# Gelu's result left in PSUM, kv's sums read from PSUM, a second exponent tile in dead weights' place, and three last blocks of 128, 384 and 256 tokens

## The chip, the cores and the metric

The kernel runs on one core of a Trainium2 chip. The core has five engines that each work through their own instructions in the order in which they were written: TensorE (PE, with its weight loads shown apart as PEld), VectorE (DVE), ScalarE (ACT), GpSimd (POOL) and SyncE (SP), which here issues the DMAs. Engines wait for each other through semaphores. SBUF is the large on-chip memory; PSUM is the small one of eight banks into which TensorE writes its products. The metric is the device time of one execution in microseconds.

## The reference: what is computed

FAVOR+ attention (random features) feeds a two-layer network. All inputs are float32, and q is drawn 4.675 times larger than k.

```python
batch, n_heads, seq, head_dim = (8, 8, 576, 64); n_features = 128
def phi(x):
    h = einsum('bhsd,md->bhsm', x, omega) - sum(x * x) / 2
    return exp(h - max(h, axis=-1)) / sqrt(m)          # x is q or k, times 64 ** -0.25
kv, z = einsum('bhsm,bhsd->bhmd', k_p, v), sum(k_p, axis=2)
num, den = einsum('bhsm,bhmd->bhsd', q_p, kv), einsum('bhsm,bhm->bhs', q_p, z) + 1e-06
x = (num / den) rearranged to 4608 tokens x 512
out = gelu(x @ w_in) @ w_out                           # 512 -> 2048 -> 512
```

## The kernel before

**Attention** goes by units: one unit is a pair of heads of one batch, so there are 32, four per batch. Its tokens sit in nine tiles of 128 for k and as four pieces of 288 columns for q. The first four units (batch 0) and the next four (batch 1) use plain float32. The 24 units of batches 2 to 7 (mode 2) use products split into a high and a low part:

- `x_high` (ACT, L295) rounds a piece of k or q, `x_low` (POOL, L301) makes the rest, `proj` and `proj_q` (PE, L308 and L336) multiply by omega into a PSUM bank of the kind `at`, of which there are three.
- For k, `proj_lo` (ACT, L313) and `proj_add` (DVE, L319, L320) add the halves into the tile `et` and take row maxima. For q, `q_blocks` (DVE, L344, L346) transposes into `et`. `k_shift` (POOL, L325) and `q_shift` (DVE, L371) subtract the maxima.
- `exps` (ACT, L379) takes the exponential of the whole of `et` in one instruction with a table load on either side of it.
- `q_back`, `q_high`, `q_low` (L386, L391, L395) transpose q's exponentials back and split them. `k_high` (POOL, L432) and `k_low` (DVE, L440) split k's into `kh` and `kl`, two buffers each, for five groups of tiles. `kv` (PE, L459) multiplies them with v, which `v_a` to `v_d` on POOL (L402, L408, L414, L420) have split into `vb`; the sums stand in one `at` bank.
- `kv_a` (ACT, L468) copies the bank's columns behind the first 64 to `kvs`; `kv_b` (DVE, L475, L476) adds the partial sums, the first time with both operands in SBUF; ACT's L477 and L483 and DVE's L487 (`kvl`) finish the weights. `num` (PE, L527), `den` (ACT, L536, L537) and `div` (DVE, L544 to L555) write the tokens into tiles `xs`.

**The network** goes by 12 blocks of 384 tokens, each in 16 chunks of 128 hidden columns. Block 0 is plain float32. For the rest, `block_max` to `block_scales` find a block's scale, and `block_high` (ACT, L687) and `block_low` (DVE, L692) split its tokens. A chunk is: `mm1` (PE, 12 matmuls at L714) into one of two `h` banks; `act_high` on ACT, Gelu from PSUM into the SBUF tile `g` (L726) and the high half `gh` (L727); `act_low` on DVE, `gl` (L732); and two chunks later `mm2` (PE, L748 to L750), nine matmuls into three `acc` banks. At a block's end `store` (DVE, L761) scales an `acc` bank into `o`, of which there are two buffers, and SP sends it out (L762).

**The order** of all this is written out by hand: every step is entered at a time `at(t, ...)`, in steps of which a chunk has six, the numbers stand in the table `X`, and a sort of the entries gives the order of the instructions on every engine. A mode-2 unit is placed every 34 to 36 steps, so about six chunks go with each; that spacing is the same before and after the change. The numbers only set an order: an engine takes its next instruction as soon as what it waits for is there.

Of the kernel before, what the change touches and what calls it, by code (L numbers as in the profile page):

```python
# [8 lines left out]
F32 = mybir.dt.float32  # L9
# [18 lines left out]
X = dict(pk=-27.0, dk=1.68, pq=-16.0, dq=2.67, xh=-4.13, xl=-2.56, plo=0.04, padd=1.37, ksh=1.5,  # L28
         qb=1.05, qm=3.26, dqm=0.12, load=-1.8, v=-14.43, dv=2.66, kh=2.57, kl=5.15, kv=6.56, dkv=1.38,
         kva=12.3, dkva=0.41, qback=7.69, qhigh=8.95, qlow=9.94, dqb=2.92, num=18.13, dnum=4.27,  # L30
         den=0.87, div=1.67, b0=110.11, b1=33.21, b2=349.2, b3=36.0, ah=4.03, al=6.26, m2=3.13,
         dm2=1.16, st=3.16, bm=-15.41, bm1=-9.64, bh=6.05, dbh=0.99, bl=2.82, m10=5.35, m11=20.5,
         mf=-13.0, mf1=4.09, mf2=7.5, mkv=5.5, mkz=7.55, mqt=8.28, mdq=1.0, mnum=17.0, mdn=4.0,
         wi=-27.37, wis=5.9, wo=5.31, wo0=0.56, wsi=72.19, wso=91.0, wss=4.24, ci=68.1, co=86.32,
         we=3.7, we0=6.27, e0=9.0, e1=2.0, e2=6.0, e3=7.3, e4=7.0, e5=10.69, lag=2, we_n=8)
# [3 lines left out]
def favor_attention_ffn(ctx: ExitStack, tc: tile.TileContext, qT, kT, v, omT, w_in, w_out, out):  # L39
# [15 lines left out]
    NTT = T // P  # L55
    NBLK = NTOK // T
# [30 lines left out]
    et = cp.tile([P, 2 * NT, M], F32, name="et")  # L87

# [225 lines left out]

    def proj_add(u, i):
        t0, t1 = XG[i][0] // P, XG[i][1] // P
        own.update({('e', t): u for t in range(t0, t1)})
        es = et[:, t0:t1]
        nc.vector.tensor_tensor(es, u.pp.pop(i)[:, 0:t1 - t0, 0], u.lo.pop(i)[:, 0:t1 - t0], op=ALU.add)  # L319
# [9 lines left out]
    ef = et.rearrange("p t m -> p (t m)")  # L329
    eq = ef[:, R2:].rearrange("p (n r) -> p n r", r=32)  # L330
# [8 lines left out]
    def q_blocks(u, g):  # L339
        own['q', g] = u  # L340
# [3 lines left out]
        nc.vector.transpose(ef[:, slice(*XG[NK + g])], u.pp.pop(NK + g)[:, 0:HS])  # L344
        s = slice(g * QB, (g + 1) * QB)
        nc.vector.tensor_reduce(u.mx[:, s], eq[:, s], axis=AX.X, op=ALU.max)  # L346
# [21 lines left out]
    def q_shift(u):  # L368
        need((u, 'nq'))
        has(u, *[('q', g) for g in range(4)])  # L370
        nc.vector.tensor_tensor(eq, eq, u.nq.unsqueeze(2).broadcast_to([P, 4 * QB, 32]), op=ALU.add)  # L371
        done.add((u, 'q'))

    def exps(u):
        if u.mode == 2:
            need((u, 'k'), (u, 'q'))
        has(u, *[('e', t) for t in range(NT)])
        has(u, *([('e', t) for t in range(NT, 2 * NT)] if u.mode == 1 else [('q', g) for g in range(4)]))
        nc.scalar.activation(et, et, AF.Exp)  # L379
# [13 lines left out]
    def q_low(u, g):  # L393
        u.ql[g] = p2().tile([P, HS], F32R, tag="ql", name="ql", bufs=4)
        (nc.gpsimd if g == 1 else nc.vector).tensor_tensor(  # L395
            u.ql[g], u.qt.pop(g), u.qh[:, g * HS:(g + 1) * HS], op=ALU.subtract)

    def v_a(u):
# [3 lines left out]
        nc.gpsimd.tensor_scalar(vb[:, :, 0:D], u.v, 1.0, 1.0, op0=ALU.mult, op1=ALU.mult)  # L402
# [7 lines left out]
    def v_c(u):  # L410
# [3 lines left out]
        nc.gpsimd.tensor_scalar(vb[:, :, D:2 * D], u.v, 1.0, 1.0, op0=ALU.mult, op1=ALU.mult)  # L414
# [10 lines left out]
    def k_high(u, g):  # L425
        need((u, 'e'))
        has(u, *[('e', t) for t in KG[g]])
        n = len(KG[g])
# [3 lines left out]
        nc.gpsimd.tensor_scalar(kh[:, :n], es, KSC, 1.0, op0=ALU.mult, op1=ALU.mult)  # L432
        u.kk[g] = (kh, kl)

    def k_low(u, g):
        has(u, *[('e', t) for t in KG[g]])
        n = len(KG[g])
        kh, kl = u.kk[g]
        es = et[:, KG[g][0]:KG[g][0] + n]
        nc.vector.scalar_tensor_tensor(kl[:, :n], es, KSC, kh[:, :n], op0=ALU.mult, op1=ALU.subtract)  # L440
        done.add((u, 'kl', g))

    def kv(u, g):
# [3 lines left out]
        has(u, 'v')  # L447
# [3 lines left out]
        kh, kl = u.kk.pop(g)  # L451
        for i, t in enumerate(KG[g]):
            for hh, ti in parts(t):
# [3 lines left out]
                ops = [(kh, VW), (kl, 2 * D + 1)]  # L457
                for x, (k, w) in enumerate(ops if f else ops[::-1]):
                    nc.tensor.matmul(o[:, 0:w], k[:, i], vb[:, ti, 0:w], start=f and x == 0, stop=end and x == 1,  # L459
# [4 lines left out]
    def kv_a(u):  # L464
        need(*[(u, 'kv', g) for g in range(len(KG))])
        u.kvs = sp.tile([P, 2, VW - D], F32, tag="kvs", name="kvs", bufs=1)
        u.pkv = u.pk[:, 0:2 * VW].rearrange("p (h w) -> p h w", h=2)
        nc.scalar.copy(u.kvs, u.pkv[:, :, D:VW])  # L468

    def kv_b(u):  # L470
# [3 lines left out]
        kz = u.kvz.rearrange("p a (b d) -> p (a b) d", d=D)  # L474
        nc.vector.tensor_tensor(kvs[:, :, 0:D], kvs[:, :, 0:D], kvs[:, :, D + 1:VW - D], op=ALU.add)  # L475
# [460 lines left out]
```

## Time and profile before

| what | value |
|---|---|
| three runs | 1087.7, 1088.22, 1088.88 us; median 1088.22 us |
| the profiled execution | 1090.31 us, its span 1088.5 us |
| mean granted TensorE clock | 0.992 |
| busy in the span | PE 1025.7, DVE 822.4, ACT 648.8, POOL 475.0 us |
| 0 to 200 us: batches 0 and 1, weights split | PE 180.05 us busy |
| 200 to 945 us: mode-2 units beside the network | PE 706.37 us, DVE 618.81 us busy |
| 945 to 1089 us: the network alone | PE 139.31 us, DVE 38.12 us busy |

A line of the profile's groups names the source line, the engine, the operation, what it writes and reads, the shape and the count; behind the bar stand the busy time in us and the mean ns of one, and then the idle time of the engine just before them with what ended it. A line of the waits names who waited, for whom, the us in total, how often, and the longest. In a table of windows each engine's busy us stands with its number of instructions, and behind them the granted TensorE clock.

### The profile page before, as it was taken

Reading aid. Unit: us, or ns where it says so; the run is one execution under the profiler, and the core shown is the slowest. Engines: PE = TensorE matmul, PEld = TensorE weight load, DVE = VectorE, ACT = ScalarE, POOL = GpSimd, SP = SyncE. Lnnn points to the kernel's source line nnn. Section 1 sums busy time; section 2 is a strip of 40 time slices with the busy share of each in tenths; the row PEclk is TensorE's granted clock in tenths of the full one; section 3 lists DMA queues with packets and bytes.
Section 4 is the critical chain, followed back from the end, with each engine's and each line's share of the span. In section 5 each row is a group of like instructions: output and inputs, shape, how many; then the busy total and the mean of one; then the engine's idle time right before and its main releaser. Section 6 shows DMA issues by size and latency. Waiting matters only on the chain.

```text
span 1088.5 us, 17164 instructions
## 1 busy us (share of the span) xinstructions
PE 1025.7 (94%) x5949; PEld 600.0 (55%) x5949; DVE 822.4 (76%) x1800; ACT 648.8 (60%) x1322; POOL 475.0 (44%) x606
## 2 busy tenths in 40 slices
PE   8999898999999799999999999899999999999998
PEld 6655454555555455555555555555555555555565
DVE  5999869987889778888887887987787898631312
ACT  7766654667666666666666666566756666633332
POOL 1233346555566545455654445565454555100000
PEclk9999999999999999999999999999999999999999
DMA  8566421221222211122221112221121220000000
GB/s 227 158 181 191 137 56 34 73 56 38 82 57 57 79 40 45 44 76 56 56 76 45 45 63 57 56 86 48 31 83 38 56 85 1 1 30 1 30 1 30
DMA packets 46278, 70.90 MB, mean 65 GB/s; under 512 B 13680, under 2 KB 22256, under 8 KB 46192
## 3 DMA queue, kind: packets, MB, share of 16 engines
q1 hardware_dynamic: 46192, 69.81, 22.5%
q8 instruction: 47, 0.77, 0.3%
q14 instruction: 39, 0.32, 0.1%
HBM read 60.36 MB, written 9.44 MB: 64 GB/s over the span
## 4 chain that ended last, share of the span: by engine, by line
PE 41%; DVE 34%; ACT 6%; issue 4%; POOL 2%; DMA 1%; DVEq 0%; POOLq 0%; ACTq 0%
PE h L714 17%; DVE gl L732 5%; PE acc L748 5%; PE acc L749 5%; PE acc L750 5%; DVE kl L440 3%; DVE ql L395 3%; ACT et L379 3%; PE at L527 3%; DVE et L319 2%; DVE nm L320 2%; DVE qt L386 2%; PE at L336 2%; DVE wil L179 2%; DVE xl L692 2%
## 5 line engine op out<-in xcount | busy, mean ns | idle before, releaser
L714 PE MATMUL h<-xl,wih 128*128 128x384 f16 x704 | 230.2, 327 | 1.5 <-DVE xl L692 1.5
L714 PE MATMUL h<-xh,wih 128*128 128x384 f16 x704 | 230.0, 327 | 0.0
L714 PE MATMUL h<-xh,wil 128*128 128x384 f16 x704 | 229.9, 327 | 0.0
L301 POOL TENSOR_TENSOR r<-xt,r 64x256 fp32r<-64x256 f32 (+2 forms) x216 | 172.5, 807 | 92.1 <-ACT r L295 77.8
L726 ACT ACTIVATE g<-h,bs 128x384 f32<-128x384 f32 x176 | 102.0, 579 | 171.2 <-PE h L714 170.6
L748 PE MATMUL acc<-woh,gh 128*128 128x512 f16 x528 | 200.6, 380 | 1.0 <-DVE o L761 1.0
L732 DVE SCALAR_TENSOR_TENSOR gl<-g,bs,gh 128x384 f16<-128x384 f32 x176 | 126.8, 721 | 97.0 <-ACT gh L727 96.2
L749 PE MATMUL acc<-woh,gl 128*128 128x512 f16 x528 | 198.9, 377 | 0.0
L750 PE MATMUL acc<-wol,gh 128*128 128x512 f16 x528 | 198.8, 377 | 0.0
L714 PEld LDWEIGHTS <-wih 128*128 128x128 f16 x1408 | 133.5, 98 | 87.8 <-issue 0.8
L432 POOL TENSOR_SCALAR kh<-et 128x256 f16<-128x256 f32 (+1 forms) x120 | 49.1, 416 | 227.4 <-ACT et L379 150.2
L727 ACT ACTIVATE gh<-g,bs 128x384 f16<-128x384 f32 x176 | 107.8, 614 | 3.3
L295 ACT CAST r<-xt 128x256 fp32r<-128x256 f32 (+2 forms) x216 | 86.3, 405 | 31.6 <-PE at L336 20.2
L714 PEld LDWEIGHTS <-wil 128*128 128x128 f16 x704 | 68.8, 98 | 47.1 <-issue 0.3
L750 PEld LDWEIGHTS <-gh 128*128 128x128 f16 x544 | 53.2, 98 | 60.0 <-issue 0.3
L159 POOL TENSOR_TENSOR w<-w,raw 128x512 int32<-128x512 int32 x32 | 42.2, 1319 | 93.2 <-DVE w L155 48.2
L386 DVE STREAM_TRANSPOSE qt<-et 128x288 f32<-128x288 f32 x96 | 44.8, 468 | 49.3 <-ACT et L379 48.8
L748 PEld LDWEIGHTS <-gh 128*128 128x128 f16 x544 | 52.9, 97 | 40.8
L440 DVE SCALAR_TENSOR_TENSOR kl<-et,kh 128x256 f16<-128x256 f32 (+1 forms) x120 | 55.3, 474 | 24.5 <-POOL kh L432 23.7
L749 PEld LDWEIGHTS <-gl 128*128 128x128 f16 x544 | 53.5, 98 | 33.9 <-issue 1.4
L308 PE MATMUL at<-om,r 128*128 128x256 f32 x216 | 61.5, 357 | 8.5 <-DVE kvz L476 8.0
L379 ACT ACTIVATE et<-et 128x2304 f32<-128x2304 f32 x28 | 59.4, 2123 | 7.6 <-DVE et L371 6.8
(173 smaller groups left out, 2002.1 us busy)
## 6 DMA issues: line engine op xcount, KB each, us to landing
xt<-in_kT SPq DMA_DIRECT2D x56, 288.0 KB, 3.8
xt<-in_qT SPq DMA_DIRECT2D x56, 288.0 KB, 3.8
v<-in_v SPq DMA_DIRECT2D x32, 320.0 KB, 3.0
out_x<-o SPq DMA_DIRECT2D x35, 256.0 KB, 2.0
raw<-in_w_in SPq DMA_DIRECT2D x16, 512.0 KB, 4.4
raw<-in_w_out SPq DMA_DIRECT2D x16, 512.0 KB, 3.6
out_x<-o SPq DMA_DIRECT2D x2, 128.0 KB, 1.7
om<-in_omT SPq DMA_DIRECT2D x2, 32.0 KB, 2.1
```

Of the source, the lines that this page charges most:

```text
L295: nc.scalar.copy(u.r[i][:, 0:b - a], xf[:, a:b])
L301: nc.gpsimd.tensor_tensor(r, xf[D:, a:b], r, op=ALU.subtract)
L379: nc.scalar.activation(et, et, AF.Exp)
L386: nc.vector.transpose(u.qt[g], ef[:, slice(*XG[NK + g])])
L440: nc.vector.scalar_tensor_tensor(kl[:, :n], es, KSC, kh[:, :n], op0=ALU.mult, op1=ALU.subtract)
L714: nc.tensor.matmul(h[:, 0:T], w, (xh, xh, xl)[k], start=(i == 0), stop=(i == 3 * NJ - 1))
L726: nc.scalar.activation(g, h[:, 0:T], AF.Gelu, scale=bsc[n][1][:, 3:4])
L727: nc.scalar.activation(gh, g, AF.Copy, scale=bsc[n][1][:, 4:5])
L732: nc.vector.scalar_tensor_tensor(gl, g, bsc[n][1][:, 4:5], gh, op0=ALU.mult, op1=ALU.subtract)
L748: nc.tensor.matmul(acc, gh[:, s], woh[:, c, c0:c1], start=(c == 0), stop=False)
L749: nc.tensor.matmul(acc, gl[:, s], woh[:, c, c0:c1], start=False, stop=False)
L750: nc.tensor.matmul(acc, gh[:, s], wol[:, c, c0:c1], start=False, stop=(c == NF - 1))
```

## The change

Five things change, and the numbers of `X` with them.

1. **Gelu in place.** For all blocks but 0, Gelu writes its result back into the `h` bank that it reads, and `gh` and `gl` read it there (L784, L785, L794 after the change). The bank is free for the next chunk but one when `gl` has been made, no longer when Gelu has been.
2. **kv's sums.** Each of the two additions of `kv_b` now has one operand in the PSUM bank (L518, L519); `kv_a` copies 65 columns per head instead of 129.
3. **Dead weights' place.** `w32`, the float32 weights, is dead once they are split and block 0 is done. A second exponent tile `et2` lies in its first half and serves every other mode-2 unit. `kh` and `kl` of a whole unit lie in its second half, in place of two buffers for each group. The tokens `xs` of blocks from the fifth on lie there too.
4. **Blocks.** Ten blocks of 384 tokens, then 128, 384 and 256. The block of 128 ends at token 3968 and needs nothing of the last batch (tokens 4032 to 4607).
5. **Engines.** The scaling at the store goes from DVE to ACT, with both factors multiplied into one beforehand; `v_a` goes from POOL to ACT.

```diff
+TBS = (384,) * 10 + (128, 384, 256)
...
+    et2 = w32f[:, 0].rearrange("p c w -> p (c w)")[:, 0:2 * NT * M].rearrange("p (t m) -> p t m", m=M)
+    NKK = -(-NT * M // 512)
+    kk = w32[:, 1].rearrange("p c w -> p (c w)")[:, 0:NT * M].bitcast(F16).rearrange("p (a t m) -> p a t m", a=2, m=M)
...
     def xs_tile(n, j):
         if (n, j) not in xs:
-            xs[n, j] = sp.tile([P, T], F32, tag="xs", name=f"xs{n}_{j}", bufs=11)
+            if n < 4:
+                xs[n, j] = sp.tile([P, T], F32, tag="xs", name=f"xs{n}_{j}", bufs=11)
+            else:
+                a, b = (T, 512) if TB[n] <= 512 - T else (0, T)
+                k = NKK + xk[a] % (NF - NKK)
...
+                xs[n, j] = w32f[:, 1, k, a:b]
...
     def v_a(u):
...
+        if X['va']:
+            nc.scalar.copy(vb[:, :, 0:D], u.v)
...
     def k_high(u, g):
...
-        kh = p2().tile([P, 2, M], F16, tag="kh", name="kh", bufs=2)
-        kl = p2().tile([P, 2, M], F16, tag="kl", name="kl", bufs=2)
-        es = et[:, KG[g][0]:KG[g][0] + n]
-        nc.gpsimd.tensor_scalar(kh[:, :n], es, KSC, 1.0, op0=ALU.mult, op1=ALU.mult)
...
+            nc.gpsimd.tensor_scalar(kk[:, 0, ts], u.et[:, ts], KSC, 1.0, op0=ALU.mult, op1=ALU.mult)
...
-        nc.vector.tensor_tensor(kvs[:, :, 0:D], kvs[:, :, 0:D], kvs[:, :, D + 1:VW - D], op=ALU.add)
-        nc.vector.tensor_tensor(kz[:, 0:4:3], u.pkv[:, :, 0:D], kvs[:, :, 0:D], op=ALU.add)
+        nc.vector.tensor_tensor(kvs[:, :, 0:D], u.pkv[:, :, 0:D], kvs[:, :, 0:D], op=ALU.add)
+        nc.vector.tensor_tensor(kn, u.pkv[:, :, 2 * D + 1:VW], kvs[:, :, 0:D], op=ALU.add)
...
     def act_high(n, c):
-        h = hs.pop((n, c))
-        g = mp[0].tile([P, T], F32, tag="g", name="g", bufs=3)
+        t = TB[n]
+        h = hs.pop((n, c))[:, 0:t]
+        g = h if X['gps'] and n else mp[0].tile([P, T], F32, tag="g", name="g", bufs=3)[:, 0:t]
...
     def store(n, i, c0=0, c1=DM):
...
+            if X['sta']:
+                nc.scalar.activation(o, acc, AF.Copy, scale=bsc[n][1][:, 6:7])
+            else:
+                nc.vector.tensor_scalar(o, acc, bsc[n][1][:, 5:6], wsc[:, 0, 2:3], op0=ALU.mult, op1=ALU.mult)
...
+            u.eb = int(u.mode == 2 and j % 2 == 0 and (b, j) != (2, 0))
+            u.et = et2 if u.eb else et
```

The switches `qsh`, `nql`, `glp`, `kzc`, `numf`, `vc` and `kha` of the new table are 0, so what hangs on them stays as it was; `sta`, `va` and `gps` are 1.

Three places show how the order moves. The first is DVE from one unit's `q_shift` to the second `gl` behind it (L371 and L395 are `q_shift`). Before:

```order
L371 TENSOR_TENSOR et<-et,nq 128x1152
L386 STREAM_TRANSPOSE qt<-et 128x288
L440 SCALAR_TENSOR_TENSOR kl<-et,kh 128x256 x2
L386 STREAM_TRANSPOSE qt<-et 128x288
L440 SCALAR_TENSOR_TENSOR kl<-et,kh 128x256
L395 TENSOR_TENSOR ql<-qt,qh 128x288
L386 STREAM_TRANSPOSE qt<-et 128x288
L732 SCALAR_TENSOR_TENSOR gl<-g,bs,gh 128x384
L440 SCALAR_TENSOR_TENSOR kl<-et,kh 128x256
L395 TENSOR_TENSOR ql<-qt,qh 128x288
L732 SCALAR_TENSOR_TENSOR gl<-g,bs,gh 128x384
```

and after the change, where `w_71` is the place of the dead weights and L479 is `k_low`:

```order
L395 TENSOR_TENSOR et<-et,nq 128x1152
L416 STREAM_TRANSPOSE qt<-et 128x288
L479 SCALAR_TENSOR_TENSOR w_71<-et,w_71 128x256 x4
L416 STREAM_TRANSPOSE qt<-et 128x288
L479 SCALAR_TENSOR_TENSOR w_71<-et,w_71 128x128
L429 TENSOR_TENSOR ql<-qt,qh 128x288
L794 SCALAR_TENSOR_TENSOR gl<-h,bs,gh 128x384
L416 STREAM_TRANSPOSE qt<-et 128x288
L429 TENSOR_TENSOR ql<-qt,qh 128x288
L794 SCALAR_TENSOR_TENSOR gl<-h,bs,gh 128x384
```

Four groups of `kl` stand in a row behind the first transpose now, and the fifth is the fifth row, ahead of both `gl`; before, three stood ahead of the first `gl`, the fourth behind it, and the fifth behind the second `gl`, past the rows shown. The second place is DVE at the end of an early block, before the change (L761 is the store's scaling):

```order
L761 TENSOR_SCALAR o<-acc,bs,wsc 128x512
L732 SCALAR_TENSOR_TENSOR gl<-g,bs,gh 128x384
L761 TENSOR_SCALAR o<-acc,bs,wsc 128x512
L344 STREAM_TRANSPOSE et<-at 128x288
L544 STREAM_TRANSPOSE rt<-dt 128x288
L346 TENSOR_REDUCE mx<-et 128x9
L545 RECIPROCAL rc<-rt 128x9
L761 TENSOR_SCALAR o<-acc,bs,wsc 128x512
L546 STREAM_TRANSPOSE rt<-rc 128x288
L344 STREAM_TRANSPOSE et<-at 128x288
L554 TENSOR_TENSOR xs_1_2445<-at,rt 64x192
```

Its counterpart after the change is on ACT, where L826 is the scaling, L784 Gelu, L785 `gh`, L585 and L586 `den` and L315 `x_high`:

```order
L784 ACTIVATE h<-h,bs 128x384
L785 ACTIVATE gh<-h,bs 128x384
L826 ACTIVATE o<-acc,bs 128x512 x2
L585 ACTIVATE dt<-at 64x288
L586 ACTIVATE dt<-at 64x288
L315 CAST r<-xt 128x288
L826 ACTIVATE o<-acc,bs 128x512
L315 CAST r<-xt 128x256
L784 ACTIVATE h<-h,bs 128x384
L785 ACTIVATE gh<-h,bs 128x384
```

The three scalings have left DVE, and ACT has two of them in a row ahead of a `den` and the third behind it, ahead of the next Gelu. The third place is DVE at kv's sums, before (L475, L476) and after (L518, L519):

```order
L395 TENSOR_TENSOR ql<-qt,qh 128x288
L475 TENSOR_TENSOR kvs<-kvs 128x2x64
L476 TENSOR_TENSOR kvz<-at,kvs 128x2x64
L319 TENSOR_TENSOR et<-at,lo 128x256
L320 TENSOR_REDUCE nm<-et 128x2
L487 TENSOR_TENSOR kvl<-kvz,kvh 128x256
L732 SCALAR_TENSOR_TENSOR gl<-g,bs,gh 128x384
```

```order
L429 TENSOR_TENSOR ql<-qt,qh 128x288
L518 TENSOR_TENSOR kvs<-at,kvs 128x2x64
L519 TENSOR_TENSOR kvz<-at,kvs 128x2x64
L344 TENSOR_TENSOR w_71<-at,lo 128x256
L345 TENSOR_REDUCE nm<-w_71 128x2
L536 TENSOR_TENSOR kvl<-kvz,kvh 128x256
L344 TENSOR_TENSOR w_71<-at,lo 128x256
L794 SCALAR_TENSOR_TENSOR gl<-h,bs,gh 128x384
```

The two sums stand at the same point of the row; what differs is that the first of them reads the PSUM bank `at`.

More of the change, by code (lines that the diff above doesn't have):

```diff
@@ L54, in favor_attention_ffn @@
     NTOK = out.shape[0]
-    NTT = T // P
-    NBLK = NTOK // T
+    TB = TBS
+    NBLK = len(TB)
+    T0 = [sum(TB[:n]) for n in range(NBLK + 1)]
+    assert T0[-1] == NTOK
     NF = F // P
```

227 lines of the change are left out of this document (141 added, 86 removed).

## The prediction

> **What bounds the kernel now.** I read the page's shares first, then the table of windows, then TensorE's waits in the long middle.
>
> ```profile
> span 1088.5 us, 17164 instructions
> PE 1025.7 (94%) x5949; PEld 600.0 (55%) x5949; DVE 822.4 (76%) x1800; ACT 648.8 (60%) x1322; POOL 475.0 (44%) x606
> ...
> 200.00:945.00 745.00, 706.37 (x4163) 414.83 (x4162) 618.81 (x1388) 481.49 (x989) 392.76 (x511) 1.00 0.20 55
> 300.00:900.00 600.00, 565.69 (x3326) 332.67 (x3324) 500.53 (x1118) 385.26 (x799) 320.69 (x418) 0.99 0.21 58
> ...
> 945.00:1089.00 144.00, 139.31 (x796) 77.72 (x794) 38.12 (x70) 45.55 (x79) 2.93 (x12) 1.00 0.05 17
> ```
>
> The columns after the length are the busy us of PE, PEld, DVE, ACT and POOL. From 945 us on PE works without a gap up to the last stores (144.0 − 139.3 = 4.7 us idle): no other engine can shorten that. From 200 to 945 us PE is idle for 745.0 − 706.4 = 38.6 us. DVE is busy there for 618.81 of 745 us (83%), so its queue runs late whenever it is held. PE's waits in this stretch, in us in total, times, longest:
>
> ```profile
> PE at L308 <- DVE kvz L476: 8.0, 14, 0.8
> PE at L527 <- DVE xs L554: 5.9, 9, 1.5
> PE at L527 <- DVE et L344: 5.3, 1, 5.3
> PE at L527 <- DVE et L319: 3.5, 6, 0.6
> PE at L336 <- POOL r L301: 2.6, 6, 0.9
> PE at L362 <- DVE sm L358: 1.9, 3, 0.8
> PE at L459 <- DVE kl L440: 1.8, 5, 0.6
> PE at L352 <- DVE mx L346: 1.6, 3, 0.8
> PE at L527 <- DVE kvl L487: 1.6, 3, 1.0
> ```
>
> Nearly all of it is PE waiting for DVE, and most for one of the three `at` banks that DVE has not emptied yet. So the bound is PE's own work plus some 38 us that DVE's lateness adds, and whatever relieves DVE in the middle can win at most about that.
>
> **The change part by part.** The sum is made on the profiled execution: 1090.31 us, its span 1088.5; the median of the three runs is 1088.22, and I take what I find off the median.
>
> *(a) kv's sums.* In the middle (300 to 900 us) DVE's groups read:
>
> ```profile
> L732 DVE SCALAR_TENSOR_TENSOR gl<-g,bs,gh 128x384 f16<-128x384 f32 x112 | 84.4, 754 | 7.2 <-ACT gh L727 6.6
> L440 DVE SCALAR_TENSOR_TENSOR kl<-et,kh 128x256 f16<-128x256 f32 x73 | 33.0, 468 | 20.6 <-POOL kh L432 20.1
> L475 DVE TENSOR_TENSOR kvs<-kvs 128x128 f32<-128x128 f32 x19 | 17.8, 936 | 0.3
> L761 DVE TENSOR_SCALAR o<-acc,bs,wsc 128x512 f32<-128x512 f32 x21 | 16.5, 792 | 5.5 <-DMA out_x<-o 5.3
> ```
>
> The first of kv's two sums (L475, both operands in SBUF) takes 936 ns on the mean. The second (L476) has the same size and reads PSUM. In ns, min/median/max of each:
>
> ```profile
> L475 DVE TENSOR_TENSOR kvs<-kvs x24: 273/799/1449, 214.0 to 938.8; 128x128 f32<-128x128 f32 x24
> L476 DVE TENSOR_TENSOR kvz<-at,kvs x24: 244/284/292, 214.8 to 939.2; 128x128 f32<-128x128 f32 x24
> ```
>
> The first varies fivefold, the second hardly. So an instruction with two SBUF operands is held up by something that an instruction with one in PSUM does not meet. The changed sum takes between 284 and 936; I take 284, −0.65 us per unit. PE's 8.0 us for `kvz` came in 14 waits of 0.57 us each, shorter than what is saved. **−7**, bounds −8 and −3.
>
> *(b) `gl`.* In the tail, where POOL is idle, the same instruction takes
>
> ```profile
> L732 DVE SCALAR_TENSOR_TENSOR gl<-g,bs,gh 128x384 f16<-128x384 f32 x35 | 21.6, 618 | 87.6 <-ACT gh L727 87.6
> ```
>
> 618 ns against 754. With `g` in PSUM it has one SBUF tensor left and should take about 618 everywhere: −0.136 × 5.9 (112 per 19 units) = −0.8 us per unit. No row has a `gl` from PSUM; bounds 618, or 629 by the 11 ns between the sums' 284 from PSUM and the best 273 from SBUF, and 754, no relief.
> [...]
>
> *(c) The scaling on ACT.* Three per 16 chunks, 21 per 19 units: DVE is rid of 21/19 × 0.792 = 0.9 us per unit. With (a) and (b): 0.65 + 0.8 + 0.9 = 2.3 us of DVE's 500.53/19 = 26.3 per unit.
>
> *(d) `kh` and `kl` without the two-buffer rotation.* Before, POOL waited for PE to consume a buffer, and DVE for POOL; over the middle:
>
> ```profile
> POOL kh L432 <- PE at L459: 67.7, 54, 2.1
> DVE kl L440 <- POOL kh L432: 23.7, 25, 1.5
> ```
>
> In the new order POOL makes all five groups in a row. Of DVE's 23.7 us most goes, 1 us per unit. So DVE is ahead by 3.3 us in 31.6 (600/19) at the point where the banks are emptied. Besides `kvz` and the one wait of 5.3, the quoted waits on DVE are 5.9 + 3.5 + 1.9 + 1.8 + 1.6 + 1.6 = 16.3 us, each at most 1.5 us long. I let two thirds go, **−11**; bounds −16 and 0. For POOL's own 2.6, with `v_a` taken off it: **−1**.
>
> *(e) The one long stall.* DVE had three scalings in its queue, the third waiting for `o`:
>
> ```profile
> 372.25 0.42 SPq L762 DMA_DIRECT2D out_x<-o  x1
> 377.45 0.81 DVE L761 TENSOR_SCALAR o<-acc,bs,wsc 128x512 f32<-128x512 f32 x1 [4.90 <-DMA out_x<-o]
> 379.06 0.61 PE L527 MATMUL at<-qh,kvh 128*128 128x288 f32 x1 [5.30 <-DVE et L344]
> ...
> 379.00:383.00 4.00, 3.94 (x13) 2.78 (x14) 2.85 (x9) 1.03 (x3) 0.00 (x0) 0.50 0.46 139
> ```
>
> A transfer issued at 372.25 let go of its buffer at 377.45; DVE stood, PE stood 5.3 us, and then ran 4 us at half the clock (0.50), 2 us more. With the scaling on ACT such a late transfer stops ACT, which stands ahead of a `den` and the next Gelu. ACT's delay comes to PE later than DVE's, since neither transposes nor divisions are behind it. I take half, **−4**; bounds −7.3 and +3 (a second one).
>
> *(f) What is added.* ACT gets the scaling and `v_a`. A 512-wide copy from PSUM and casts from SBUF take
>
> ```profile
> L505 ACT COPY qh<-at 128x512 f32<-128x512 f32 x10 | 5.9, 599 | 4.6 <-PE at L498 4.6
> ...
> L295 ACT CAST r<-xt 128x288 fp32r<-128x288 f32 x76 | 32.3, 432 | 1.5 <-PE at L336 1.4
> ...
> L295 ACT CAST r<-xt 128x256 fp32r<-128x256 f32 x76 | 30.3, 404 | 18.1 <-PE at L336 14.6 <-POOL r L301 1.7 <-POOL vb L420 1.4
> ```
>
> so 21/19 × 0.6 + (0.432 + 352 × 0.875 ns = 0.74) = 1.4 us on 385.26/19 = 20.3 per unit, 69% of the period. It has room, but `v_a` stands between `kvs` and what follows it: **+1**, bounds 0 and +8. The `h` bank is held until `gl` is done. Around a unit's exponentials, when Gelu is latest:
>
> ```profile
> 549.37 0.33 PE L714 MATMUL h<-xl,wih 128*128 128x384 f16 x1
> ...
> 551.68 0.58 ACT L726 ACTIVATE g<-h,bs 128x384 f32<-128x384 f32 x1
> ...
> 553.75 0.42 DVE L440 SCALAR_TENSOR_TENSOR kl<-et,kh 128x256 f16<-128x256 f32 x1 [1.45 <-POOL kh L432]
> ...
> 554.98 0.72 DVE L732 SCALAR_TENSOR_TENSOR gl<-g,bs,gh 128x384 f16<-128x384 f32 x1
> ...
> 557.16 0.33 PE L714 MATMUL h<-xh,wih 128*128 128x384 f16 x1
> ```
>
> the chunk ends at 549.70, its `gl` at 555.70, and the bank is written anew at 557.16: 1.46 us to spare. In the new order two more `kl` (0.94 us) and one transpose less (about 0.47) stand ahead of that `gl`, and the wait of 1.45 goes. So about 2 us are to spare, and the hold costs nothing; without that cover it is the slower rival. In the tail a chunk starts every 3.9 us by the chain,
>
> ```profile
> 1073.34 1.95 PE h L714 x12
> 1077.24 1.95 PE h L714 x12
> ```
>
> and Gelu, `gh` and `gl` take less than 2 together (0.58, 0.61, 0.62), so there is no hold there either.
>
> *(g) Small blocks.* PE's work in the last blocks is the same 768 tokens. A matmul of 128 columns could cost more than a third of one of 384; kv's of 129 columns start the next one 0.06 us later:
>
> ```profile
> 588.36 0.22 PE L459 MATMUL at<-vb,kl 128*128 128x129 bf16 x1
> 588.42 0.25 PE L459 MATMUL at<-vb,kh 128*128 128x193 bf16 x1
> ```
>
> against a third of 1.95/12 = 0.1625 that 384 columns take (0.054): at most 192 × 0.006 = 1.2 us. ACT's and DVE's fixed costs come 16 times more; chunks of 1.3 us (12 × 0.06, and 3 × 1.95/9 for the second product) leave ACT with the block before's three scalings behind: **+2**, bounds 0 and +6. That this block needn't wait for the last batch answers no wait in the list: 0. The second `et` and the tokens' new place remove waits that the lists don't show: 0. The split of the weights before 200 us moves a little: 0, bounds ±3.
>
> Some waits of the weight loads lie inside PE's "busy" time, the one for `kl` among them:
>
> ```profile
> PEld L459 <- DVE kl L440: 8.8, 23, 0.9
> ```
>
> I take half of it, **−4**, bounds −8.8 and 0. Sum: −7 − 11 − 1 − 4 + 1 + 2 − 4 = **−24: 1064 us.**
>
> **The rivals.**
> *More than that:* every quoted wait goes and the stall with it, −8 − 16 − 3 − 7 − 6 for the weight loads = −40: 1048. For it: 3.3 us of relief against waits of at most 1.5. Against it: PE's order and spacing hardly change, and a faster PE meets the next late thing.
> *Nothing to speak of:* DVE is earlier, but what it waits for (ACT's exponentials, ACT's `den`) isn't, so PE's waits only change names; kvz alone goes, and the added costs eat it: −7 + 1 + 2 = −4, 1084, or with (f) at its +8 1091; 1087 between them. For it: DVE's idle time of 17% shows that it too waits.
> *Slower, the `h` bank:* if `gl` comes more than those 1.46 us later than today relative to PE (ACT held by scaling and `v_a`, Gelu behind the exponentials), PE stops at the first matmul of the chunk after next in each of 24 units. At 1.5 us beyond the point it costs 36 us and turns −24 into +12: 1100. It decides where two chunks' Gelu stand behind a table load. Against it: the wait of 1.45 us for `kh`, gone.
>
> **How the numbers follow.** Forecast 0.62, own range 1053 to 1076; more 0.14; nothing 0.11; the `h` bank 0.13. No change means within 0.2% (2.2 us), about what can be told here. Faster is the forecast, the larger gain, and 0.04 of the rest: 0.80; same 0.08; slower 0.12, nearly all of it the bank. The range 1046 to 1087 reaches to the larger gain and to all but the end of "nothing"; some 0.2 are left out.
>
> **What would show it.** Right: both kv sums under 0.3 us; `gl` near 0.62 to 0.68 in the middle as in the tail; no wait of DVE for `o`; `kl` not waiting for `kh`; PE idle from 200 to 945 us down to about 15 to 20. Wrong: PE waiting at the first matmul of a chunk for `gl`; ACT waiting for a store's transfer for microseconds; half clock anywhere past 150 us; or PE's idle time as large as now under other names.

## The result, and the profile after

| | before | changed |
|---|---|---|
| runs, us | 1087.96 median (1086.67 to 1088.88, 4 runs) | 1038.51 median (1037.87 to 1040.48, 4 runs) |
| profiled execution, its span, us | 1090.31, 1088.5 | 1037.87, 1036.1 |

The ratio is 0.9549, 95% interval 0.9532 to 0.9566: 49.5 us less, where the forecast was 24 less. The time lies below the range (1046 to 1087). The sign and the place were right, the size was not.

The page's shares after, the span first:

```profile
span 1036.1 us, 17688 instructions
PE 1011.4 (98%) x6144; PEld 610.2 (59%) x6144; DVE 764.2 (74%) x1798; ACT 678.3 (65%) x1419; POOL 449.8 (43%) x600
```

The windows after. The columns are start and end, length, the busy us of PE, PEld, DVE, ACT and POOL, the granted clock, DMA share and GB/s:

```profile
0.00:200.00 200.00, 185.75 (x1029) 109.14 (x1030) 168.80 (x356) 130.34 (x264) 79.47 (x87) 0.99 0.48 141
200.00:900.00 700.00, 693.12 (x4173) 416.98 (x4172) 567.03 (x1382) 493.38 (x1040) 366.93 (x501) 1.00 0.20 58
900.00:1036.00 136.00, 132.50 (x945) 84.12 (x943) 28.41 (x62) 54.59 (x116) 3.45 (x14) 1.00 0.05 18
```

In the middle PE now idles 6.9 us of 700, where it idled 38.6 of 745. The waits of PE there, in us in total, times, longest:

```profile
PE at L376 <- DVE mx L370: 2.1, 4, 0.9
PE at L217 <- DVE cm L213: 1.5, 2, 0.7
PE at L328 <- DVE et L344: 0.6, 2, 0.3
PE at L224 <- DVE ct L221: 0.4, 1, 0.4
```

Of the nine waits that the prediction quotes, five are gone altogether: `kvz`, both for `et` at `num`, POOL's `r` and `kvl`. Three are small now (the division 0.4 us in all, `sm` 0.3, `kl` 0.2), and one stays, the wait for `mx`, q's row maxima (1.6 us at L352 before, 2.1 at L376 now). Where the time went can be read at two marks. The first matmul of block 1 starts at 187.7 us before and at 180.7 after (−7.0); that of block 10 at 955.8 and at 901.8 (−54.0, so −47.0 between the two marks); the last stretch gives 1.6 back, to the span's −52.4.

PE's idle time fell by 38.1 us over the whole span (62.8 to 24.7). The other 14 are inside what the profile calls busy. The windows between the two marks show it, since both kernels do the same matmuls there:

```profile
187.71:955.79 768.08, 726.49 (x4260) 425.58 (x4259) 639.62 (x1429) 493.27 (x1014) 402.48 (x525) 1.00 0.19 54
180.71:901.76 721.05, 712.18 (x4260) 426.37 (x4259) 586.61 (x1415) 507.59 (x1064) 376.93 (x512) 1.00 0.20 58
```

The same 4260 matmuls were 726.5 us "busy" before and are 712.2 now. Of these 14.3 us, 2.0 are the matmuls at half clock behind the long stall, which the prediction counts there. The other 12.3 fit waits of the weight loads that the modelled ends of matmuls had swallowed: PE's weight loads waited 8.8 us for `kl`, 8.0 for POOL's `r` and 10.6 for POOL's `v` before, and after the change the first two read 0.5 us each and the third is gone.

The two sums of `kv_b` and `gl` after, in ns min/median/max:

```profile
L518 DVE TENSOR_TENSOR kvs<-at,kvs x24: 247/292/294, 207.0 to 885.9; 128x128 f32<-128x128 f32 x24
L519 DVE TENSOR_TENSOR kvz<-at,kvs x24: 252/282/292, 207.5 to 886.2; 128x128 f32<-128x128 f32 x24
...
L794 DVE SCALAR_TENSOR_TENSOR gl<-h,bs,gh x141: 570/608/621, 201.8 to 898.8; 128x384 f16<-128x384 f32 x141
```

No `gl` takes over 621 ns any more. The same view of `gl` before:

```profile
L732 DVE SCALAR_TENSOR_TENSOR gl<-g,bs,gh x140: 570/620/1475, 200.1 to 941.1; 128x384 f16<-128x384 f32 x140
```

The prediction went by the mean, 754 against 618. The median is 620, so most `gl` lost nothing; 54 of the 140 took over 0.7 us, and the longest lost 0.86. The timeline of before shows one (start, us, engine, line, operation; in brackets idle time before it and who ended it):

```profile
849.05 1.42 POOL L420 TENSOR_TENSOR vb<-v,vb 128x640 bf16<-128x640 f32 x1
...
849.48 1.41 DVE L732 SCALAR_TENSOR_TENSOR gl<-g,bs,gh 128x384 f16<-128x384 f32 x1 [0.23 <-ACT gh L727]
...
850.80 0.61 DVE L319 TENSOR_TENSOR et<-at,lo 128x256 f32<-128x256 f32 x2
851.27 0.40 PE L527 MATMUL at<-qh,kvh 128*128 128x288 f32 x1 [0.58 <-DVE et L319]
...
851.97 0.40 ACT L537 ACTIVATE dt<-at 64x288 f32<-64x288 f32 x1 [0.84 <-PE at L527]
```

POOL's instruction ends at 849.05 + 1.42 = 850.47 and `gl` at 849.48 + 1.41 = 850.89, 0.42 us later. `gl` took 0.79 us more than its 0.62, the next addition came that much later, PE stood 0.58 us, and then ACT 0.84. This picture recurs at 433.96, 499.21, 594.85, 688.46 and 753.87 us with the same numbers: these are the six waits of 0.6 us that the prediction quoted as `PE at L527 <- DVE et L319: 3.5`. The picture is general: every `gl` over 0.7 us in the kernel before (55 of them) ends 0.40 to 0.42 us behind the end of an instruction on POOL.

### The profile page after: what moved, and what is told of

Same layout as the page of the kernel before. It is cut to its first block, busy times and chain, and to the rows that moved or that the text cites. A ratio compares the mean times of both kernels' runs of the same rounds, so it can differ in the third digit from the quotient of the medians.

```text
span 1036.1 us, 17688 instructions
## 1 busy us (share of the span) xinstructions
PE 1011.4 (98%) x6144; PEld 610.2 (59%) x6144; DVE 764.2 (74%) x1798; ACT 678.3 (65%) x1419; POOL 449.8 (43%) x600
## 4 chain that ended last, share of the span: by engine, by line
PE 72%; DVE 9%; ACT 4%; POOL 3%; issue 1%; DMA 1%; POOLq 0%; DVEq 0%; ACTq 0%
PE h L771 28%; PE acc L812 9%; PE acc L813 9%; PE acc L814 9%; PE at L576 3%; PE at L497 3%; PE at L328 2%; PE acc L806 2%; PE h L756 2%; PE at L359 2%; DVE xl L745 1%; DVE gl L794 1%; POOL woh L186 1%; DVE mx L370 1%; ACT et L403 1%
## 5 line engine op out<-in xcount | busy, mean ns | idle before, releaser
L771 PE MATMUL h<-xl,wih 128*128 128x384 f16 (+2 forms) x768 | 238.1, 313 | 1.2 <-DVE xl L745 1.2
L771 PE MATMUL h<-xh,wih 128*128 128x384 f16 (+2 forms) x768 | 237.9, 313 | 0.4 <-DVE gl L794 0.4
L771 PE MATMUL h<-xh,wil 128*128 128x384 f16 (+2 forms) x768 | 237.9, 313 | 0.0
L784 ACT ACTIVATE h<-h,bs 128x384 f32<-128x384 f32 (+2 forms) x192 | 101.4, 529 | 160.2 <-PE h L771 152.1
L812 PE MATMUL acc<-woh,gh 128*128 128x512 f16 (+1 forms) x528 | 199.9, 379 | 0.0
L813 PE MATMUL acc<-woh,gl 128*128 128x512 f16 (+1 forms) x528 | 198.4, 376 | 0.1
L814 PE MATMUL acc<-wol,gh 128*128 128x512 f16 (+1 forms) x528 | 198.4, 376 | 0.0
L794 DVE SCALAR_TENSOR_TENSOR gl<-h,bs,gh 128x384 f16<-128x384 f32 (+2 forms) x192 | 110.4, 577 | 105.0 <-ACT gh L785 104.0
L785 ACT ACTIVATE gh<-h,bs 128x384 f16<-128x384 f32 (+2 forms) x192 | 106.4, 557 | 3.5
L315 ACT CAST r<-xt 128x256 fp32r<-128x256 f32 (+2 forms) x216 | 85.7, 416 | 24.3 <-PE at L359 16.9
L497 PE MATMUL at<-vb,w 128*128 128x129 bf16 (+1 forms) x480 | 54.6, 234 | 0.2 <-DVE w L479 0.2
```

The costliest lines, as they stand in the source:

```text
L315: nc.scalar.copy(u.r[i][:, 0:b - a], xf[:, a:b])
L497: nc.tensor.matmul(o[:, 0:w], kk[:, k, t], vb[:, ti, 0:w], start=f and x == 0, stop=end and x == 1, skip_group_check=True)
L771: nc.tensor.matmul(h[:, 0:TB[n]], w, (xh, xh, xl)[k], start=(i == 0), stop=(i == 3 * NJ - 1))
L784: nc.scalar.activation(g, h, AF.Gelu, scale=bsc[n][1][:, 3:4])
L785: nc.scalar.activation(gh, g, AF.Copy, scale=bsc[n][1][:, 4:5])
L794: nc.vector.scalar_tensor_tensor(gl, g, bsc[n][1][:, 4:5], gh, op0=ALU.mult, op1=ALU.subtract)
```

## The experiments

"Against the changed kernel" is (ratio − 0.9549) × 1088 us, each ratio being to the kernel before on the same chip. With both intervals it is known to about ±2.5 us (±3 for `no_kk`, ±5 for `three_busy`). The theories have letters in the expectations: A, DVE's lateness held the banks and each relief gives a part; B, the new numbers give nearly all; L, every us of DVE's work counts; P, POOL's and ACT's time counts; and, from `three_busy` on, C, DVE's delay counts only at one place of the unit. Two things hold for all of them. An edit also shifts the order of instructions a little: without `gl`, `ql` and the scalings, DVE's row has 1534 instructions in the traces, and from none (`no_et2`, `pool_two`) to 337 (`no_four`) of them stand in another place than in the changed kernel. And each version meets its own late stores: the longest wait of ACT for a store's buffer is 1.8 us in the changed kernel and 1.8 to 5.2 in the versions that scale on ACT. A single difference carries both.

### One part undone at a time

Gelu's result back in SBUF:

```diff
-         ... vc=0, kha=0, gps=1)
+         ... vc=0, kha=0, gps=0)
```

> The changed kernel with Gelu's result back in an SBUF tile g. Theory A (DVE's lateness held the at banks; every part that takes load off DVE gives a share): gl in the middle goes from about 0.61 back to 0.72 to 0.75 us, 0.8 us of DVE per unit come back, and the time rises by 3 to 12 us over 1038.5, since DVE is busy 81% of the middle here too. Theory B (the order's new numbers give nearly all of it): gl longer, time within 3 us of 1038.5. Theory H (the bank held until gl is a cost): faster than 1038.5 by more than 2 us.

1056.58 us (1055.85 to 1059.92), ratio 0.9711 [0.9691, 0.9732]: **+17.6 us**, above all that was expected. Its `gl`:

```profile
L794 DVE SCALAR_TENSOR_TENSOR gl<-g,bs,gh x141: 569/618/2234, 203.7 to 918.6; 128x384 f16<-128x384 f32 x141
```

Again the median is as it was, and the maximum is 2.23 us. That one in the timeline:

```profile
391.96 2.11 POOL L350 TENSOR_TENSOR et<-et,nm 128x1152 f32<-128x1152 f32 x1
...
392.25 2.23 DVE L794 SCALAR_TENSOR_TENSOR gl<-g,bs,gh 128x384 f16<-128x384 f32 x1
```

POOL's subtraction ends at 394.07, `gl` at 394.48, 0.41 us behind it, as 0.42 in the kernel before. All 40 `gl` over 0.7 us in this run end 0.40 to 0.42 us behind an instruction of POOL.

The first sum from two SBUF operands:

```diff
-        nc.vector.tensor_tensor(kvs[:, :, 0:D], u.pkv[:, :, 0:D], kvs[:, :, 0:D], op=ALU.add)
+        nc.vector.tensor_tensor(kvs[:, :, 0:D], kvs[:, :, 0:D], kvs[:, :, D + 1:VW - D], op=ALU.add)
```

> The changed kernel with kv's first sum back on two SBUF operands (and 129 columns copied by ACT). Theory A: the first sum takes 0.8 to 0.9 us again instead of under 0.3, PE waits at the projection of k for kvz some 8 us again, and the time rises by 5 to 14 us over 1038.5. Theory B: the sum is slow again, time within 3 us.

1046.34 us (1045.3 to 1049.45), ratio 0.9616 [0.9596, 0.9637]: **+7.3 us**, the very size of the forecast's −7, but not by its mechanism. The sum itself hardly grows, its median by 2 ns; only a few are long, since in the changed kernel's order it seldom meets an instruction of POOL (the six over 0.39 us end 0.15 us behind one). In ns min/median/max:

```profile
L518 DVE TENSOR_TENSOR kvs<-kvs x24: 251/294/783, 207.6 to 893.4; 128x128 f32<-128x128 f32 x24
```

What is new are late stores, in the waits of ACT and PE in its middle (ACT's were 2.1 us in the changed kernel, PE's none):

```profile
ACT o L826 <- DMA out_x<-o: 12.4, 4, 5.0
...
PE acc L812 <- ACT o L826: 4.9, 2, 2.7
```

The scaling of the stores back on DVE:

```diff
-         ... sta=1, ...
+         ... sta=0, ...
```

> The changed kernel with the store's scaling back on DVE, at the new places in the order. Theory A: 0.9 us of DVE per unit come back, +3 to +12 us; a wait of DVE for the transfer of o shows again, once long at most. Theory B: within 3 us. If a late transfer of o was the large item of the gain, a stall of PE of about 5 us with half clock behind it shows again in this run, and is absent from the changed kernel.

1042.19 us (1041.76 to 1043.26), ratio 0.9575 [0.956, 0.959]: **+2.8 us**, for 34 instructions, 32 of them of 0.8 us.

`kh` and `kl` in two rotating buffers for each group, as before:

```diff
-            nc.gpsimd.tensor_scalar(kk[:, 0, ts], u.et[:, ts], KSC, 1.0, op0=ALU.mult, op1=ALU.mult)
+        kh = p2().tile([P, 2, M], F16, tag="kh", name="kh", bufs=2)
+        kl = p2().tile([P, 2, M], F16, tag="kl", name="kl", bufs=2)
+        nc.gpsimd.tensor_scalar(kh[:, :n], u.et[:, ts], KSC, 1.0, op0=ALU.mult, op1=ALU.mult)
```

> The changed kernel with kh and kl back in two rotating buffers, the order as in the changed kernel (five kh in a row on POOL, four kl in a row on DVE). Theory A: POOL waits for PE between kh, DVE for kh some 20 us or more in all; with four kl ahead of everything else on DVE the delay is passed on to gl and the banks: +8 to +25 us. Theory B: within 3 us.

1047.94 us (1045.87 to 1050.23), ratio 0.963 [0.9605, 0.9655]: **+8.8 us**. DVE waits 26.1 us for `kh` again, and one store comes 4.5 us late.

`v_a` back on POOL:

```diff
-         ... numf=0, va=1, ...
+         ... numf=0, va=0, ...
```

> The changed kernel with v's cast back on POOL (24 of 0.75 us, 18 us moved from ACT to POOL). Theory C and my forecast's step for POOL: +0 to +4 us, 1039 to 1043. Theory P (POOL's time counts): +10 or more.

1048.64 us (1046.86 to 1049.8), ratio 0.9624 [0.9609, 0.9639]: **+8.2 us**, more than theory C and less than theory P. In its trace ACT waits 8.2 us for two stores, the longest 5.03. SyncE's queue and ACT at that place:

```profile
362.27 0.33 SPq L303 DMA_DIRECT2D v<-in_v  x1
...
362.65 0.90 SPq L829 DMA_DIRECT2D out_x<-o  x2
...
366.38 0.69 ACT L826 ACTIVATE o<-acc,bs 128x512 f32<-128x512 f32 x1 [5.03 <-DMA out_x<-o]
```

The same queue in the changed kernel:

```profile
356.83 0.93 SPq L829 DMA_DIRECT2D out_x<-o  x2
358.72 0.60 SPq L302 DMA_DIRECT2D xt<-in_qT  x1
359.65 0.33 SPq L829 DMA_DIRECT2D out_x<-o  x1
362.30 0.60 SPq L302 DMA_DIRECT2D xt<-in_qT  x1
362.95 0.59 SPq L303 DMA_DIRECT2D v<-in_v  x1
```

In `no_va` the load of the next `v` stands ahead of the two stores in SyncE's queue. It is issued at 362.27, just when POOL's last reader of `v` ends (360.88 + 1.36 = 362.24); the stores wait behind it though their scalings were done at 360.04, and the third scaling waits for their buffer. In the changed kernel the stores stand ahead of that load. How much of the 8.2 us is this stall and how much POOL's 18 us isn't settled.

The second `et` left out, and, as another version, twelve blocks of 384 tokens (with the last chunk's `gl` at its old time):

```diff
-            u.eb = int(u.mode == 2 and j % 2 == 0 and (b, j) != (2, 0))
+            u.eb = 0
...
-TBS = (384,) * 10 + (128, 384, 256)
+TBS = (384,) * 12
```

> The changed kernel with one exponent tile for all units. Theory A: the order is the same and no wait in the trace of before named a write into et held by a reader, so within 3 us of 1038.5. Theory C (the second tile lets the next unit's work start before the last one's is read): +10 us or more, with POOL or DVE waiting at writes into et.

> The changed kernel with twelve blocks of 384 tokens (the last chunk's gl at its old place). Theory A: within 3 us of 1038.5, the end differing by less than 2 us. Theory D (the last blocks' cut gives a good part): +5 us or more, with PE idle around the last unit's division and before the block after it.

1042.48 us (1041.28 to 1044.56), ratio 0.9571 [0.9556, 0.9586], +2.4 us, which these runs don't tell from nothing; and 1040.03 us (1037.79 to 1040.86), ratio 0.9543 [0.9528, 0.9558], −0.7 us: the small blocks do nothing.

### The numbers

The changed kernel with the old table `X` (the switches as in the new one), and the kernel before with the new table (the last chunk's `gl` at its old time):

```diff
-X = dict(pk=-27.05, dk=1.68, pq=-16.0, ...       # old_numbers; the reverse in numbers_alone
+X = dict(pk=-27.0, dk=1.68, pq=-16.0, ...
```

> The changed kernel's structure with the order's numbers of before (the table X of before, the new switches as in the change). Theory A (the structure relieves DVE): at most a third of the gain is lost, 1040 to 1055. Theory B (the numbers give nearly all of it): 1070 to 1090.

> The kernel before with the new numbers alone (the last chunk's gl kept at its old place, since the end needs it). Theory A: 1078 to 1098, no large gain without relief for DVE. Theory B: below 1060.

1051.0 us (1049.33 to 1053.69), ratio 0.9649 [0.9631, 0.9668], and 1095.45 us (1094.54 to 1096.67), ratio 1.0058 [1.0041, 1.0075]. The structure alone gives 38 us (1 − 0.9649 of 1088), the numbers alone lose 6; on the new structure they are worth 10.9. Theory B is out.

### Several parts, and one part alone

All four reliefs of DVE undone together: the diffs of `no_gps`, `no_kvs`, `no_sta` and `no_kk` in one.

> The changed kernel with its numbers, but all four of DVE's reliefs undone together: Gelu's result in SBUF, the first sum from two SBUF operands, the scaling of the stores on DVE, kh and kl in two rotating buffers. Singly they cost 17.6, 7.3, 2.8 and 8.8 us, 36.5 in all. Theory L (each is DVE time on the path, so they add up): +33 to +45, 1072 to 1084. Rival S (they overlap: any one of them makes DVE late, the next costs less): +15 to +25, 1054 to 1064.

1073.02 us (1071.88 to 1074.3), ratio 0.9859 [0.9843, 0.9875]: **+33.7 us**, against 36.5 for the four singly. Theory S is out, and the numbers add up within their errors. The causes need not: `no_kvs` and `no_kk` hold late stores, and here PE waits 7.2 us for the scaling on DVE (two waits), which `no_sta` alone doesn't show.

Gelu in PSUM as the only edit of the kernel before:

```diff
-        g = mp[0].tile([P, T], F32, tag="g", name="g", bufs=3)
+        g = h[:, 0:T] if n else mp[0].tile([P, T], F32, tag="g", name="g", bufs=3)
```

> The kernel before with one edit: Gelu writes its result into its PSUM bank (but for block 0) and gh and gl read it there; the order of the numbers, the sums, the scalings, kh and kl as before. Theory L: DVE is rid of 144 x 0.14 = 20 us, the middle gets shorter by nearly that: -14 to -20 us against the kernel before, 1069 to 1075. Theory B (the gain needs the new order of numbers): within 4 us of the kernel before. Theory H (with the old order the h bank is held too long, since gl is later there): slower than before by 5 or more.

1056.83 us (1054.93 to 1058.28), ratio 0.9709 [0.969, 0.9727]: **31.7 us less than before** by this one line, where theory L had at most 20. TensorE's waits in its middle:

```profile
PE at L527 <- DVE et L344: 3.4, 1, 3.4
...
PE at L527 <- DVE xs L554: 1.3, 4, 0.4
PE at L527 <- DVE et L319: 1.3, 2, 0.6
```

The 8.0 us of `kvz` are gone, and 3.5 and 5.9 have become 1.3 and 1.3. The first sum still has two operands in SBUF and still varies from 288 to 1452 ns, but it got shorter too, from 840 to 587 ns on the mean. In the six units where PE had waited some 0.77 us for `kvz` it took 1.44 to 1.45 us before and takes 0.32 to 0.33 now; in two others it still takes 1.45, and PE doesn't wait. Like the long `gl`, the long sums end just behind an instruction of POOL (all over 0.4 us by 0.14 to 0.15 us). So this edit also moved the sums away from POOL's instructions, and the 31.7 us hold more than `gl`'s own 20; how much is which isn't settled.

### Amount or place

`gl` in two pieces (256 and 128 columns) in ten of sixteen chunks: DVE's total grows by 20.1 us (846.0 to 866.1, all instructions of the trace summed), nearly as much as by Gelu in SBUF (868.7), but evenly and with nothing else touched. `split_gh` does the same to `gh` on ACT, with the same loop around its line.

```diff
+            for ps in (((0, 256), (256, 384)) if TB[n] == 384 and c % 3 else ((0, TB[n]),)):
+                s = slice(*ps)
+                nc.vector.scalar_tensor_tensor(gl[:, s], g[:, s], bsc[n][1][:, 4:5], gh[:, s], op0=ALU.mult, op1=ALU.subtract)
```

> The changed kernel with the split's low half (gl) made in two instructions of 256 and 128 columns instead of one of 384 in ten of the sixteen chunks of each full block; the same values. In the tail the rows read 484 + 350 = 834 ns for the two pieces against 618 for one, so each split chunk puts 0.216 us more on DVE: 90 such chunks in blocks 1 to 9, 19.4 us, as much as 144 chunks at 743 - 608 = 135 ns lost when Gelu went back to SBUF (+17.6 us). [...] Theory L (the middle is paced by DVE's amount of work, nearly one to one): +15 to +20 us against the changed kernel, 1054 to 1059. [...]

> The changed kernel with the high half (gh) on ACT made in two instructions of 256 and 128 columns in the same ten chunks of each full block; the same values. By the tail's rows 473 + 366 - 580 = 0.259 us more on ACT for each, 90 chunks, 23.3 us. Theory L (DVE's amount of work paces the middle, ACT at 72% has room): +0 to +6 us. Theory P (ACT's time counts as much, so part of the 17.6 us was ACT's 33 + 23 ns per chunk): +12 to +23.

1039.18 us (1038.03 to 1040.32), ratio 0.9548 [0.9532, 0.9564]: **−0.1 us**; theory L, which had 15 to 20, falls. `split_gh`: 1044.14 us (1043.44 to 1044.34), ratio 0.9592 [0.9576, 0.9608]: +4.7 us for 23 us on ACT.

Then three pieces of 128 columns in 40 chunks of blocks 1 to 9: once those 40 whose `gl` had taken over 0.7 us in `no_gps` (30 of them 12 to 21 us behind the start of a unit's exponentials), once 40 others (within 8 us behind them or past 24). The edit differs only in the list of chunks:

```diff
+THREE = {16, 19, 21, 22, ...}      # three_busy; {18, 24, 28, 34, ...} in three_quiet
```

> The changed kernel with gl made in three pieces of 128 columns (3 x 338 - 607 = 0.407 us more each) in exactly those 40 chunks of blocks 1 to 9 whose gl took over 0.7 us when Gelu went back to SBUF; 16.3 us on DVE in all, nothing else touched. Most of them lie 12 to 24 us behind a unit's exponentials. Theory C (what counts is DVE's delay at that place, where PE waits for the banks it empties): +10 to +18 us against the changed kernel, 1049 to 1057. Theory P (POOL's own stretching by 16 us, or ACT's, made the 17.6 us): at most +4, 1043 or less.

> The same three pieces in 40 other chunks of blocks 1 to 9, which lie within 8 us behind a unit's exponentials or more than 24 us behind them; the same 16.3 us on DVE. Theory C: at most +3 us, 1042 or less. Theory L (amount): as three_busy.

1046.63 us (1044.14 to 1053.31), ratio 0.9614 [0.9571, 0.9658]: **+7.1 us**; 1039.11 us (1037.8 to 1043.67), ratio 0.9546 [0.9522, 0.9569]: **−0.3 us**. The same 16.3 us on DVE cost 7 where the long `gl` had stood and nothing elsewhere. In its trace `three_quiet` even has the larger sum of DVE's instructions (868.7 us against 861.6), but PE's waits from 200 to 920 us are 6.6 us against 10.0. The first is less than the 10 to 18 expected, and its runs spread widely; the two intervals just part.

POOL's low half of the tokens in two instructions in two of nine groups, 13.3 us on POOL:

```diff
-        nc.gpsimd.tensor_tensor(r, xf[D:, a:b], r, op=ALU.subtract)
+        m = b - P if i in (2, 7) else a
+        for x, y in ((a, m), (m, b)):
+            if x < y:
+                r = u.r[i][D:, x - a:y - a]
+                nc.gpsimd.tensor_tensor(r, xf[D:, x:y], r, op=ALU.subtract)
```

> The changed kernel with POOL's low half of the tokens made in two instructions in two of the nine groups of each unit (513 + 513 - 748 = 0.28 us more each, 48 of them: 13.3 us on POOL; its total grew by 16 us when Gelu went back to SBUF, 9 of them in these instructions). Theory P: +8 to +15 us, 1047 to 1054. Theory C: at most +4, 1043 or less (POOL is busy for 54% of the middle).

1041.29 us (1039.59 to 1043.35), ratio 0.9559 [0.9543, 0.9575]: +1.1 us. POOL's stretching is hardly the main thing.

So of the 17.6 us, DVE's delay at that place accounts for some 8, give or take 5 (7.1 × 18.5/16.3, the 40 long `gl` having lost 18.5 us), and POOL's 16 and ACT's 8.5 us of added time for some 1.3 and 1.7 by the rates of `pool_two`, which is within the noise, and `split_gh`. The other 6 or 7 aren't shown. What the pieces don't imitate is the size of single delays: 0.41 us each here, up to 1.6 in `no_gps`; and 0.21 us each in `split_gl`, which hit 23 of the same 40 chunks, cost nothing. That small delays are absorbed and long ones are not would fit, but was not tried by itself.

### Two attempts at more

The second cast of `v` on ACT as well, and, as another version, all four `ql` on DVE:

```diff
-         ... va=1, vc=0, ...
+         ... va=1, vc=1, ...
...
-         nql=0, ...
+         nql=3, ...
```

> The changed kernel with the second cast of v (24 of 0.76 us on POOL) made on ACT as well. Theory P2 (POOL's amount of work still costs, as v's first cast seems to say): -4 to -10 us against the changed kernel, 1029 to 1035. Theory Q (POOL has room now, and ACT, 62% to 72% busy, pays for it as it paid 5.6 us for 23 us of split gh): 0 to +5, 1038 to 1044.

> The changed kernel with the fourth of the four low halves of the queries (ql) on DVE like the other three (24 of 0.55 us, 13 us) instead of on POOL (24 of 0.80, 19 us). They lie 6 to 12 us behind the exponentials, ahead of the place where DVE's delay counts. Theory P2: -4 to -8 us. Theory C and Q (DVE's time counts only where PE waits for its banks): between -2 and +5, 1037 to 1044.

1055.67 us (1054.65 to 1056.35), ratio 0.97 [0.9686, 0.9715], **+16.4 us**, beyond both theories; and 1043.28 us (1041.27 to 1046.66), ratio 0.9589 [0.9564, 0.9614], +4.4 us, with one late store (ACT waits 5.2 us). Taking more work off POOL wins nothing here. Of `vc_act`, the waits of TensorE and then of ACT in the middle:

```profile
PE at L576 <- DVE et L368: 5.4, 3, 2.1
PE at L376 <- DVE mx L370: 3.6, 5, 1.2
```

```profile
ACT vb L452 <- POOL v L445: 10.4, 7, 1.9
```

A wait that POOL had served in its own order now stands in ACT's queue, and what is behind it on ACT (`den`, Gelu) comes late. That this delay reaches PE through DVE fits the two lists and isn't shown further; ACT also waits 7.4 us for two stores, and PE 2.6 us for the scaling behind them. No version beat the changed kernel by more than can be measured.

## Why the prediction was wrong

**The bound** was named rightly: PE's own work plus DVE's lateness in the middle, and nothing to win in the tail. Its limit was not. "Some 38 us" counted the idle time, and some 12 more lay in PE's busy time.

**(b) `gl`** was right in its size, 608 to 618 ns from PSUM at every place, and wrong in what that size is worth; this is the step that failed. "−0.136 × 5.9 = −0.8 us per unit" spread the relief evenly, put it beside `kh` and the scaling, and let "two thirds" of the short waits go. In `no_gps` 40 of the 144 `gl` of blocks 1 to 9 have 18.5 of the 18.9 us, most of them 12 to 21 us behind the start of the exponentials. PE's waits follow: 13.3 of its 17.3 us from 200 to 920 us of that run fall 18 to 27 us behind the same starts, where DVE empties the banks. Undone, the edit costs 17.6 us; alone it gives 31.7 on the old order, more than the whole forecast.

All 95 `gl` over 0.7 us in the kernel before and in `no_gps`, where Gelu's result lies in SBUF, end 0.40 to 0.42 us behind POOL's instruction, and the one from PSUM is never held (621 ns at most in the changed kernel). That the loss sits in single instances could have been read from the trace of before, where the maximum is 1475 ns beside a median of 620. What in POOL's instruction holds `gl` is not shown. Nor does any run show the 0.68 us up to which the prediction put `gl` from PSUM: in the tail it is 618 ns before, from SBUF, and 618 after, from PSUM.

**(a) the sums**: 287 and 280 ns on the mean where 284 was taken. But PE's 8.0 us for `kvz` go with Gelu's edit already, and in `no_kvs` the sum stays short while PE waits 4.9 us behind late stores. That `no_kvs` costs 7.3 where the forecast had −7 is chance.

**(c) the scaling**: −0.9 us of DVE per unit came; undone, it costs 2.8 us.

**(d) `kh` and `kl`**: DVE's wait for `kh` went, as said. It was not free: POOL now makes all `kh` in a row, beside `kl`, and the four wide `kl` of a unit got longer, from 468 ns to

```profile
L479 DVE SCALAR_TENSOR_TENSOR w<-w 128x256 f16<-128x256 f32 x42 | 21.9, 574 | 0.4
...
L479 DVE SCALAR_TENSOR_TENSOR w<-et,w 128x256 f16<-128x256 f32 x40 | 20.4, 563 | 0.3
```

so 0.4 of that one us per unit came back as length (4 × 0.1), while the fifth, of 128 columns, fell from 508 to 243 ns. In `no_kk`, with the old buffers and the new order, the wide ones take 469 to 477 ns again. Undone, this part costs 8.8 us, one late store among them. For (a) to (d) together the forecast had −7, −11 and −1 for POOL, 19 in all; undone together they cost 33.7.

**(e) the long stall**: gone, with its half clock: −7.3, the bound, where −4 was taken. The transfer that comes late is not gone from the design. The sentence "such a late transfer stops ACT" came true in `no_kvs`, `no_kk`, `no_va`, `ql_dve` and `old_numbers` (4.5 to 5.2 us each time), for 3.2 to 3.8 us in six other versions, and not in the changed kernel, where ACT waits 2.1 us in all.

**(f) what is added**: ACT's busy time grew by 29.5 us, and PE's list of waits has nothing of it; the `h` bank holds PE once in the whole program, for 0.4 us. The rival of the slower kind had its wait, but not its price. For `v_a` off POOL the forecast had −1; undone it costs 8.2.

**(g) small blocks**: 0 instead of +2. The second `et`, put at 0, is at 2.4 ± 2.5. The first 187 us, put at 0 ± 3, gave 7. Some 3 of them are the granted clock of the first 150 us (0.97 in the profile before, 0.99 after), which also differs among versions with the same start (in the second fortieth of the span it is under 0.9 in `no_gps`, `split_gl` and `three_busy`, and 0.9 or more in the changed kernel and in `no_va`). The rest goes with the numbers: at granted clocks of 0.997 and 0.994 over the whole runs block 1 starts at 184.8 us in `gps_alone`, with the old numbers, and at 181.3 in `numbers_alone`, with the new.

**The weight loads**: −4 for waits hidden in "busy", bounds −8.8 and 0. PE's busy time between the two marks fell by 14.3 with equal matmuls, 12.3 without the half clock. Half of the wait for `kl` was too little: nearly all of it went, and the waits of other weight loads with it.

Of "what would show it", every sign of "right" came, and PE's idle time went past the 15 to 20 it named, to 6.9. The rival "more than that" had the mechanism (nearly every quoted wait goes) and 1048; what it lacks is most of the hidden waits, for which it had 6, and the start.

## What to carry to other kernels

Ask for the minimum, median and maximum of an instruction, not for its mean: where the median equals the undisturbed time and the maximum is twice it, as with `gl` here (620 and 1475 ns, 618 undisturbed), some of the instances carry the whole loss, and its price depends on where they stand (+7.1 us in `three_busy`, −0.3 in `three_quiet`). Here an instruction that was held behind another engine's delayed what was queued behind it (in the kernel before `gl` by 0.79 us at 849.48 us, then PE by 0.58 and ACT by 0.84): some 20 us of `gl` (0.14 on the mean) were worth 17.6 us when put back and 31.7 when taken out alone, together with what else that moved, and 20 us of work spread evenly were worth nothing. In `no_va`, where two stores stood behind a load in SyncE's queue, they waited for what the load waited for: scaled at 360.04 us, they were issued at 362.65, behind the load at 362.27.

## What was not expected of the hardware

- `gl` and kv's first sum, each with two SBUF tensors, were held behind instructions of POOL, and where they were held they ended a fixed time behind them: `gl`, which takes 0.62 us alone, 0.40 to 0.42 us (2.23 us in all at worst, in `no_gps`), and the sum, which takes 0.28 alone, mostly 0.14 to 0.15 us (1.45 at worst, before and in `gps_alone`). With one operand in PSUM they took at most 0.62 and 0.29 us in the changed kernel.
- From PSUM into PSUM Gelu takes 556 ns on the mean, from PSUM into SBUF 580; `gh` from PSUM 584, from SBUF 614. `gl` takes 618 ns in the tail from either.
- The same 4260 matmuls of TensorE were busy for 726.5 us before and for 712.2 after. Of the 14.3 us, 2.0 are half clock; the rest fits waits that the modelled ends hide.
